# Indirect transfers tied one by one to TensorE's products, at the seam between a retention stage and a mixture of experts

## The chip, the core and the metric

The kernel runs on one core of a Trainium2 chip. The metric is device time of one execution in microseconds (us). The core has TensorE (PE, matrix products), VectorE (DVE), ScalarE (ACT), GpSimd (POOL) and SyncE (SP, which here issues DMAs); each runs its own instructions in order and waits on semaphores for the others.

## What is computed

Retention (a decaying causal attention) over 8 batches, 8 heads, 576 positions and 64 wide heads, then a mixture of 8 experts on its 4608 rows of 512, in which each row goes to the one expert with the largest gate.

```python
scores = np.matmul(q, k.transpose(0, 1, 3, 2)) / np.sqrt(64)
rel = pos[:, None] - pos[None, :]
Dmat = np.where(rel >= 0, gamma[:, None, None] ** rel[None], 0.0)     # gamma per head
x = rows(np.matmul(scores * Dmat, v))                                 # 4608 x 512
e_idx = np.argmax(x @ w_gate, axis=1)
gate_w = softmax(x @ w_gate)[chosen]; eom = sigmoid(x @ w_output_gate)
for e in range(8):
    mask = e_idx == e
    out[mask] = gate_w[mask, None] * eom[mask, e, None] * (np.maximum(x[mask] @ w1[e], 0) @ w2[e])
```

## The kernel before

The instructions of each engine stand in the order in which the code is written; a framework adds the semaphores.

**First stage.** A loop runs over 36 tiles of 128 rows (`g`). For a tile TensorE does, in this order: `scores(g + 1)` for the next tile (L439), sometimes `ranks` of a gate group (L529 to L536), `out_x(g)`, which is 16 products of the state with q (L470, here "state products") and then 16 of v with the masked scores (L473, "value products"), `update(g)` of the state (L456), `k_rows(g + 1)` (transposes of k, L417), and every fourth tile the `logits` of a group of four tiles (L491). ScalarE copies the results out (xT at L476, stT at L458, kn at L424), DVE masks the scores (L443) and transposes x for storing (L481).

Four tiles make a gate group `n`: DVE's `gate_a` (from L497 to L518, the one-hot of the chosen expert), then TensorE's `ranks`, DVE's `gate_b`, `gate_d`, `gate_c`. The last group's run behind the loop.

**GpSimd's list.** GpSimd prepares q (`prep_q`, L403) and v (`prep_v`, L410) of tiles some steps ahead. Between these it issues indirect DMAs: for every finished gate group four `scatter`s (L575, one for each tile, behind a small memset at L574), which write each token's entry into its expert's list `lst` in DRAM, and twelve `gather`s (L190), which fetch x of expert 0's first three token tiles (`w2h`, `w2l` are the buffers that they borrow) by the parts of the list that are already there. Scatters wait in a Python list `todo`; the tables `puts` and `mine` (L660, L661) say how many scatters and gathers are written into which tile's code; they have no tie to TensorE. In the expert stage, gathers (`paced`) wait for the product that was written last before them.

**The seam.** Behind the loop: logits of the last group, `store_x`, `load_idx(0, TA, TA + 1)` (SyncE's load L335 of a part of expert 0's list, which waits for all scatters so far), `gate_a` and `exp_a`, `mm1(0, 0, 0)`, which is the first of eight blocks of 12 products of expert 0 (L242), `ranks`, the rest of the gate, the last four scatters, `mm1(0, 0, 1)` and the sorting of the experts.

**Expert stage.** For each of 8 experts blocks `mm1` (L242) and `mm2` or `mm2t` (L263, L289), in float32 split into a high and a low part (three products for one). Results are written by GpSimd's indirect DMAs (L248).

Of the kernel before, what the change touches and what calls it, by code (L numbers as in the profile page):

```python
# [19 lines left out]
SYNC = mybir.DependencyInfo(mybir.DependencyClass.Sync, mybir.DependencyReason.DATA)  # L20
# [16 lines left out]
TA, CT = 3, 5  # L37
# [14 lines left out]
def tile_retention_moe(  # L52
# [126 lines left out]
        xps.append(a[:, 1].rearrange("p (k n) -> p k n", k=KB))  # L179
    pools = {"xt0": xta, "ht0": hpa}  # L180

    last = [None]

    def gather(e, t, u, paced=False):
        if u == 0 and e == 0 and t < TA:
            make_gidx(0, t, t + 1, G)
        if u == 0 and (e, t) not in XG:
            XG[e, t] = pools["xq"].tile([P, 4, P], F32, name="x_q")
        seen = xs if e or t >= TA else xs[0:4 * P * (READY[t] + 1) * GT]
        i = G.indirect_dma_start(out=XG[e, t][:, u, :], out_offset=None, in_=seen,  # L190
                                 in_offset=bass.IndirectOffsetOnAxis(ap=gidx[:, e, 4 * t + u:4 * t + u + 1], axis=0))
        if paced:
            tc.add_manual_dep(i.ins, last[0].name, SYNC, reason="one gather to a stretch of products")

    def size(e, part):
        return N1[e] if part else R0[e]
# [19 lines left out]
    def transp_a(e, t):  # L216
        src = xps.pop(0) if xps else pools["xq"].tile([P, KB, P], F32, name="x_t", bufs=2)
        nu = columns(e, t)
        V.transpose(out=src.rearrange("p k (u j) -> p u k j", u=4)[:, 0:nu],  # L219
                    in_=XG[e, t].rearrange("p u (k i) -> p u k i", k=KB)[:, 0:nu])  # L220
        part, c0, n = where(e, t)
        hi, lo = (a[:, :, c0:c0 + n] for a in xt_of(e, part))
        A.copy(out=hi, in_=src[:, :, 0:n])  # L223
        return lambda: V.tensor_tensor(out=lo, in0=src[:, :, 0:n], in1=hi.bitcast(F32), op=ALU.subtract)  # L224
# [236 lines left out]
    def out_x(g, S_sb, state):  # L461
        c = g % CPB
        o = o_ps[:, :, 256 * (g % 2):256 * (g % 2) + 256]
        part = lambda p, r: o[64 * ((p + r) % 2):64 * ((p + r) % 2) + 64, r, P * (p // 2):P * (p // 2) + P]
        order = [(p, (p + i) % 2) for p in range(NP) for i in range(2)]
        if state is not None:
            w = 64 if c == 4 else P
            for p, r in order:
                s = slice(64 * r, 64 * r + 64)
                T.matmul(part(p, r)[:, 0:w], lhsT=state[s, p, :], rhs=qs[g][s, p, 0:w],  # L470
                         start=(p < 2), stop=False, skip_group_check=True)
        for p, r in order:
            T.matmul(part(p, r), lhsT=vs[g][:, 2 * p + r, :], rhs=S_sb[:, r, p, :],  # L473
                     start=(state is None and p < 2), stop=True, skip_group_check=True)
        xT[g] = wk.tile([P, KB, P], F32, name="xT", bufs=6)
        A.copy(out=xT[g].rearrange("p (r s) i -> p r s i", r=2),  # L476
               in_=o[:, :, :].rearrange("p r (s i) -> p r s i", s=2))

    def x_rows(g):
        xq = xr[g] = wk.tile([P, 4, P], F32, name="xq", bufs=3)  # L480
        V.transpose(out=xq.rearrange("p b (r s i) -> p r s b i", r=2, s=2),  # L481
                    in_=xT[g].rearrange("p (r s) (b j) -> p r s b j", r=2, b=4))
# [81 lines left out]
    def gate_c(n):  # L564
        zs, sli = gt["zs"], gt["sli"]
        es = gt["ps"][:, 396:400].rearrange("p (t e) -> p t e", t=GT)
        V.tensor_reduce(out=es, in_=gt["ex"], op=ALU.add, axis=AX.X)
        V.tensor_scalar(out=es, in0=es, scalar1=1e-9, scalar2=None, op0=ALU.add)
        V.scalar_tensor_tensor(out=zs, in0=zs, scalar=1.0, in1=es, op0=ALU.add, op1=ALU.mult)
        ent = ents[:, n * GT:(n + 1) * GT]  # L570
        V.reciprocal(out=ent.bitcast(F32)[:, :, 1:2], in_=zs)  # L571

        def scatter(t):
            G.memset(tick, 0.0)  # L574
            i = G.indirect_dma_start(out=lst, out_offset=bass.IndirectOffsetOnAxis(ap=sli[:, t, :], axis=0),  # L575
                                     in_=ent[:, t], in_offset=None)
            tc.declare_no_dep(i.ins, group="lst", reason="the slots of all tokens differ")
            tc.add_to_no_dep_group("lst", i.ins)
            scat.append(i.ins)

        todo.extend(partial(scatter, t) for t in range(GT))
# [51 lines left out]
    for g in range(NTILE):  # L633
# [23 lines left out]
            ranks(n)  # L657
            exp_a(n)
        lead = 3 if g > 6 else 2
        puts = {16: 2, 17: 2, 18: 0, 19: 0, 24: 2, 25: 2, 27: 2, 28: 2, 30: 0, 31: 0, 35: 5}.get(g, 1)  # L660
        mine = {23: 1, 24: 1, 25: 1, 26: 1, 28: 1, 29: 2, 30: 1, 31: 1, 32: 1, 33: 2}.get(g, 0)  # L661
        while min(ready) < min(g + lead + 1, NTILE):
            if ready[0] <= ready[1]:
                prep_q(ready[0])
# [20 lines left out]
        out_x(g, S_sb, prev)  # L685
        if g == NTILE - 1:
            last_x = transp_a(0, 2)
        x_rows(g)
        if lows and late in (0, 3):
            lows.pop(0)()  # L690
# [22 lines left out]
    psctx.close()  # L713
    pools["ps_h"] = mctx.enter_context(tc.tile_pool(name="ps_h", bufs=5, space=PSUM, side="right", reuse_waits="tile"))
    store_x(NTILE - 1)
    load_idx(0, TA, TA + 1)
    gate_a(NG - 1)
    exp_a(NG - 1)
    mm1(0, 0, 0)
    ranks(NG - 1)  # L720
    gate_b(NG - 1)
    exp_b(NG - 1)
# [341 lines left out]
```

## Time and profile before

| | |
|---|---|
| median of 3 runs | 588.22 us (586.67 to 591.13) |
| profiled execution | 594.7 us, its span 592.6 us |
| TensorE (PE) busy | 558.9 us, 94% of the span |
| VectorE (DVE) busy | 367.0 us, 62% |
| GpSimd (POOL) busy | 329.7 us, 56% |
| ScalarE (ACT) busy | 179.0 us, 30% |
| mean granted TensorE clock | 0.980 |

Busy shares are means over both stages. The profile's rows give times from the start of the span. In a row of a timeline, the bracket at the end is the idle time of that engine just before the instruction and what released it: an instruction of another engine, "issue" where nothing that the profile shows was waited for, "remote" where a semaphore was waited for whose sender can't be named.

### The profile page before, as it was taken

The numbers are of one execution on the slowest core, as the hardware profiler recorded it, in microseconds if no ns is written. First come the engines' busy times: TensorE is split into PE (matmuls) and PEld (weight loads), VectorE is DVE, ScalarE is ACT, GpSimd is POOL, SyncE is SP. The second block draws the span as 40 slices with busy tenths as digits, with TensorE's granted clock in tenths as the row PEclk, the third lists the DMA queues.
The fourth block names the chain that finished last, engine by engine and source line by source line (L and its number), as shares of the span: only waits on it lengthen the run. The fifth ranks groups of instructions, "written<-read, shape, count | busy, mean of one in ns | idle before, by whom it ended". The sixth has DMA issues, their size and how long they took to land. (4 is left out here: it accounts for less than half of the span.)

```text
span 592.6 us, 14974 instructions
## 1 busy us (share of the span) xinstructions
PE 558.9 (94%) x5886; PEld 519.0 (88%) x5886; DVE 367.0 (62%) x805; ACT 179.0 (30%) x419; POOL 329.7 (56%) x359
## 2 busy tenths in 40 slices
PE   6989998999769989999999999999999999999994
PEld 4878887778569989998999899899999989999993
DVE  3668887678547465884576378457636747755440
ACT  4524435566114122420421232042123204213011
POOL 3848886889454576664555264345527526624602
PEclk9989998999879999999999999999999999999999
DMA  8989987796102475645643664464356455543123
GB/s 335 363 294 324 299 294 251 232 322 205 59 25 70 132 206 177 207 147 146 193 151 106 189 202 132 112 221 158 113 178 213 141 145 167 166 124 130 45 56 114
DMA packets 50069, 105.86 MB, mean 179 GB/s; under 512 B 10190, under 2 KB 24719, under 8 KB 49998
## 3 DMA queue, kind: packets, MB, share of 16 engines
q1 hardware_dynamic: 40254, 84.53, 44.8%
q0 software_dynamic: 9312, 19.71, 10.3%
q8 instruction: 47, 0.77, 0.5%
q10 hardware_dynamic: 432, 0.66, 0.4%
q14 instruction: 24, 0.20, 0.1%
HBM read 79.67 MB, written 25.33 MB: 177 GB/s over the span
## 5 line engine op out<-in xcount | busy, mean ns | idle before, releaser
L190 POOL DMA_INDIRECT x_q<-xs,gidx x139 | 149.4, 1075 | 90.2 <-PE y_ps L289 36.5
L242 PE MATMUL h_ps<-xh,w1h 128*128 128x256 f32 (+5 forms) x512 | 154.1, 301 | 0.4 <-DVE hl L245 0.4
L242 PE MATMUL h_ps<-xl,w1h 128*128 128x256 f32 (+5 forms) x512 | 153.9, 301 | 0.3 <-DVE xl L224 0.3
L242 PE MATMUL h_ps<-xh,w1l 128*128 128x256 f32 (+5 forms) x512 | 153.7, 300 | 0.0
L242 PEld LDWEIGHTS h_ps<-xh,w1h 128*128 128x128 f32 x512 | 97.2, 190 | 1.3 <-DVE hl L245 0.7
L242 PEld LDWEIGHTS h_ps<-xl,w1h 128*128 128x128 f32 x512 | 97.1, 190 | 0.8 <-DVE xl L224 0.5
L242 PEld LDWEIGHTS h_ps<-xh,w1l 128*128 128x128 f32 x512 | 97.9, 191 | 0.0
L244 ACT ACTIVATE hh<-h_ps 128x256 fp32r<-128x256 f32 (+5 forms) x128 | 52.4, 415 | 134.9 <-PE h_ps L242 110.0
L245 DVE SCALAR_TENSOR_TENSOR hl<-h_ps,hh 128x256 fp32r<-128x256 f32 (+5 forms) x128 | 57.8, 458 | 51.9 <-ACT hh L244 41.5
L289 PE MATMUL y_ps<-hh,w2l 128*128 128x360 f32 (+3 forms) x256 | 81.2, 317 | 0.0
L289 PE MATMUL y_ps<-hl,w2h 128*128 128x360 f32 (+3 forms) x256 | 81.2, 317 | 0.0
L289 PE MATMUL y_ps<-hh,w2h 128*128 128x360 f32 (+3 forms) x256 | 81.2, 317 | 0.0
L443 DVE TENSOR_TENSOR S_sb<-sc,cmat_sb 128x512 f32<-128x512 f32 x72 | 45.9, 679 | 22.7 <-PE sc L439 21.0
L223 ACT CAST xh<-x_t 128x512 fp32r<-128x512 f32 (+4 forms) x36 | 21.3, 592 | 122.3 <-DVE x_t L219 84.8
L224 DVE TENSOR_TENSOR xl<-x_t,xh 128x512 fp32r<-128x512 f32 (+4 forms) x36 | 23.8, 660 | 53.5 <-ACT xh L223 51.1
L248 POOL DMA_INDIRECT out_dram<-y,idx x15 | 15.3, 1018 | 67.1 <-ACT y L272 60.4
L248 POOL DMA_INDIRECT out_dram<-yr,idx x24 | 26.7, 1113 | 44.1 <-ACT yr L315 42.5
L439 PE MATMUL sc<-pk 64*64 64x64 f32 (+1 forms) x1152 | 38.4, 256 | 12.6 <-issue 7.2
L439 PEld LDWEIGHTS sc<-pk 64*64 64x64 f32 x1152 | 30.6, 139 | 21.5 <-issue 20.0
L167 DVE TENSOR_TENSOR w1l<-st,w1h 128x1024 fp32r<-128x1024 f32 (+1 forms) x36 | 47.9, 1330 | 2.1
L263 PE MATMUL y_ps<-w2h,hl 128*128 128x512 f32 x120 | 46.8, 390 | 2.0 <-DVE hl L245 2.0
L575 POOL DMA_INDIRECT lst<-ents,sli x36 | 37.0, 1029 | 20.6 <-DVE ents L571 15.0
(137 smaller groups left out, 970.1 us busy)
## 6 DMA issues: line engine op xcount, KB each, us to landing
st<-in_w_dram SPq DMA_DIRECT2D x64, 512.0 KB
pk<-in_pack_dram SPq DMA_DIRECT2D x35, 768.0 KB
xs<-xq SPq DMA_DIRECT2D x36, 256.0 KB
yr<-yg SPq DMA_DIRECT2D x16, 256.0 KB
yg<-yt SPq DMA_DIRECT2D x16, 176.0 KB
x_q<-xs,gidx POOLq DMA_INDIRECT x139
yg<-yt SPq DMA_DIRECT2D x12, 160.0 KB
yr<-yg SPq DMA_DIRECT2D x4, 208.0 KB
```

The lines of the kernel that those rows point to most:

```text
L167: V.tensor_tensor(out=lo[:, k], in0=st[:, k], in1=hi[:, k].bitcast(F32), op=ALU.subtract)
L190: i = G.indirect_dma_start(out=XG[e, t][:, u, :], out_offset=None, in_=seen, in_offset=bass.IndirectOffsetOnAxis(ap=gidx[:, e, 4 * t + u:4 ...
L224: return lambda: V.tensor_tensor(out=lo, in0=src[:, :, 0:n], in1=hi.bitcast(F32), op=ALU.subtract)
L242: last[0] = T.matmul(ps, lhsT=a[:, k, :], rhs=b[:, k, :], start=(j == 0), stop=(j == 3 * KB - 1)).ins
L244: A.activation(out=hh, in_=ps, func=AF.Relu)
L245: V.scalar_tensor_tensor(out=hl, in0=ps, scalar=0.0, in1=hh.bitcast(F32), op0=ALU.max, op1=ALU.subtract)
L248: i = G.indirect_dma_start(out=out, out_offset=bass.IndirectOffsetOnAxis(ap=rows, axis=0), in_=y, in_offset=None, bounds_check=NT - 1, oob ...
L263: last[0] = T.matmul(ps, lhsT=a[:, c0:c0 + n], rhs=b, start=(j == 0), stop=(j == 3 * FB - 1)).ins
L289: last[0] = T.matmul(ps[:, 0:n], lhsT=a, rhs=b, start=(j == 0), stop=(j == 3 * FB - 1)).ins
L439: T.matmul(sc[r][64 * h:64 * h + 64, p, i], lhsT=pk[g][s, 1, P * p + 64 * h:P * p + 64 * h + 64], rhs=qs[g][s, p, i], start=True, stop=Tru ...
L443: V.tensor_tensor(out=S_sb[:, r].rearrange("p (a b) i -> p a b i", a=2), in0=sc[r].rearrange("p (a b) i -> p a b i", a=2), in1=m, op=ALU.mult)
L575: i = G.indirect_dma_start(out=lst, out_offset=bass.IndirectOffsetOnAxis(ap=sli[:, t, :], axis=0), in_=ent[:, t], in_offset=None)
```

## The change

Three things are changed in the code.

- `gather` and `scatter` can be tied to a product: they then wait for its semaphore. `out_x` keeps its last state product as `marks["q"]` and its last value product as `marks["v"]`.
- The tables: a scatter more is written into tile 31 and none into tiles 33 to 35; the two gathers of tile 33 leave the table. Instead, behind `out_x(33)` come the two gathers, one tied to each mark, and behind `out_x(34)` and `out_x(35)` two scatters each, tied in the same way.
- Behind the loop, two scatters are issued from within `mm1(0, 0, 0)`, tied to its first and its seventh product, and `load_idx(0, TA, TA + 1)` stands behind that block. The four scatters of the last group are as before.

```diff
-    def gather(e, t, u, paced=False):
+    def gather(e, t, u, paced=False, by=None):
...
-        if paced:
-            tc.add_manual_dep(i.ins, last[0].name, SYNC, reason="one gather to a stretch of products")
+        if paced or by:
+            tc.add_manual_dep(i.ins, (by or last[0]).name, SYNC, reason="one gather to a stretch of products")
...
-                T.matmul(part(p, r)[:, 0:w], lhsT=state[s, p, :], rhs=qs[g][s, p, 0:w],
-                         start=(p < 2), stop=False, skip_group_check=True)
+                marks["q"] = T.matmul(part(p, r)[:, 0:w], lhsT=state[s, p, :], rhs=qs[g][s, p, 0:w],
+                                      start=(p < 2), stop=False, skip_group_check=True).ins
...
-            T.matmul(part(p, r), lhsT=vs[g][:, 2 * p + r, :], rhs=S_sb[:, r, p, :],
-                     start=(state is None and p < 2), stop=True, skip_group_check=True)
+            marks["v"] = T.matmul(part(p, r), lhsT=vs[g][:, 2 * p + r, :], rhs=S_sb[:, r, p, :],
+                                  start=(state is None and p < 2), stop=True, skip_group_check=True).ins
...
-        def scatter(t):
+        def scatter(t, by=None):
             G.memset(tick, 0.0)
...
+            if by:
+                tc.add_manual_dep(i.ins, (by[0] if by is last else by).name, SYNC,
+                                  reason="one scatter to a stretch of products")
...
-        puts = {16: 2, 17: 2, 18: 0, 19: 0, 24: 2, 25: 2, 27: 2, 28: 2, 30: 0, 31: 0, 35: 5}.get(g, 1)
-        mine = {23: 1, 24: 1, 25: 1, 26: 1, 28: 1, 29: 2, 30: 1, 31: 1, 32: 1, 33: 2}.get(g, 0)
+        puts = {16: 2, 17: 2, 18: 0, 19: 0, 24: 2, 25: 2, 27: 2, 28: 2, 30: 0, 33: 0, 34: 0, 35: 0}.get(g, 1)
+        mine = {23: 1, 24: 1, 25: 1, 26: 1, 28: 1, 29: 2, 30: 1, 31: 1, 32: 1}.get(g, 0)
...
         out_x(g, S_sb, prev)
         if g == NTILE - 1:
             last_x = transp_a(0, 2)
+        if g == 33:
+            gather(0, *divmod(got, 4), by=marks["q"])
+            gather(0, *divmod(got + 1, 4), by=marks["v"])
+        elif g > 33:
+            for m in "qv":
+                todo.pop(0)(by=marks[m])
         x_rows(g)
...
     store_x(NTILE - 1)
-    load_idx(0, TA, TA + 1)
     gate_a(NG - 1)
     exp_a(NG - 1)
-    mm1(0, 0, 0)
+    todo[:] = [partial(f, by=last) for f in todo]
+    mm1(0, 0, 0, (1, 7))
+    load_idx(0, TA, TA + 1)
     ranks(NG - 1)
```

The order of TensorE's, DVE's and ScalarE's instructions stays. On GpSimd, this stood between the preparation of tile 34 and that of the last gate (L403 and L410 are prep_q and prep_v of tile 35, L190 gathers, L575 scatters; the words in brackets are the semaphores waited for, PE for TensorE, DMASW for earlier indirect DMAs):

```order
L410 TENSOR_TENSOR pk<-pk,gkf 128x192
L403 TENSOR_TENSOR pk<-pk,gq_sb 128x512 [waits PE_49,Activation_49]
L190 DMA w2l_107<-xs,gidx 128x128 [waits DMASW1_49]
L410 TENSOR_TENSOR pk<-pk,gkf 128x192
L574 MEMSET tick 128x1
L575 DMA lst<-ents,sli 37888x16 [waits DMASW2_49,DVE_49]
L190 DMA w2l_107<-xs,gidx 128x128 [waits DMASW3_49]
L190 DMA w2l_107<-xs,gidx 128x128 [waits DMASW4_49]
L574 MEMSET tick 128x1 [waits Pool_49]
L575 DMA lst<-ents,sli 37888x16 [waits DMASW5_49]
```

and this stands there now:

```order
L410 TENSOR_TENSOR pk<-pk,gkf 128x192
L574 MEMSET tick 128x1
L575 DMA lst<-ents,sli 37888x16 [waits DMASW1_49,DVE_49]
L403 TENSOR_TENSOR pk<-pk,gq_sb 128x512 [waits PE_49,Activation_49]
L190 DMA w2l_107<-xs,gidx 128x128 [waits DMASW2_49]
L410 TENSOR_TENSOR pk<-pk,gkf 128x192
L574 MEMSET tick 128x1 [waits Pool_49]
L575 DMA lst<-ents,sli 37888x16 [waits DMASW3_49]
L190 DMA w2l_107<-xs,gidx 128x128 [waits DMASW4_49,PE_49]
L190 DMA w2l_107<-xs,gidx 128x128 [waits DMASW5_49,PE_49]
```

A scatter has moved ahead of prep_q of tile 35, and the two gathers of tile 33 now wait for TensorE as well.

Further down GpSimd's list, from the second of the scatters of tile 34 on, now tied (L559 is a small update of the list bases):

```order
L575 DMA lst<-ents,sli 37888x16 [waits DMASW7_49,PE_49]
L559 TENSOR_TENSOR base_81<-csm_sb,bump 128x1 [waits DVE_49]
L574 MEMSET tick 128x1 [waits Pool_49]
L575 DMA lst<-ents,sli 37888x16 [waits DMASW0_49,DVE_49,PE_49]
L574 MEMSET tick 128x1 [waits Pool_49]
L575 DMA lst<-ents,sli 37888x16 [waits DMASW1_49,PE_49]
L574 MEMSET tick 128x1 [waits Pool_49]
L575 DMA lst<-ents,sli 37888x16 [waits DMASW2_49,PE_49]
L574 MEMSET tick 128x1 [waits Pool_49]
L575 DMA lst<-ents,sli 37888x16 [waits DMASW3_49,PE_49]
```

The first of these five scatters belongs to tile 34, the next two to tile 35, the last two to `mm1(0, 0, 0)`. In the kernel before, the same five stood behind L559 with no wait for PE.

## Rows read from the trace of the kernel before

**Rows 1.** Busy time by stretch: stretch, us, PE, PEld, DVE, ACT, POOL busy, PEclk, DMA share, GB/s

```profile
177.00:592.60 415.60, 405.14 (x2636) 389.50 (x2634) 247.15 (x500) 99.50 (x205) 203.81 (x197) 1.00 0.49 148
150.90:157.00 6.10, 3.05 (x34) 1.78 (x34) 2.24 (x8) 1.00 (x3) 3.78 (x6) 0.95 0.22 68
162.80:171.10 8.30, 3.64 (x44) 2.93 (x45) 3.10 (x10) 1.61 (x4) 5.13 (x10) 0.94 0.13 47
171.10:176.90 5.80, 5.77 (x24) 5.72 (x24) 3.35 (x16) 0.68 (x2) 2.25 (x5) 0.50 0.03 7
```

**Rows 2.** PE's waits from 176.9 to the end, longest: total us, times, longest

```profile
PE y_ps L263 <- DVE hl L245: 2.0, 1, 2.0
```

**Rows 3.** PE in order of time: start us, us, line, operation, [idle before <-releaser]

```profile
109.55 1.09 PE L473 MATMUL o_ps<-S_sb,pk 128*64 128x128 f32 x16
...
115.80 1.09 PE L473 MATMUL o_ps<-S_sb,pk 128*64 128x128 f32 x16
...
148.81 1.11 PE L473 MATMUL o_ps<-S_sb,pk 128*64 128x128 f32 x16 [0.29 <-issue]
...
150.90 0.79 PE L439 MATMUL sc<-pk 64*64 64x128 f32 x12
152.10 0.32 PE L439 MATMUL sc<-pk 64*64 64x64 f32 x3 [0.41 <-issue]
...
156.48 0.56 PE L439 MATMUL sc<-pk 64*64 64x64 f32 x8 [0.99 <-issue]
156.97 0.21 PE L529 MATMUL lg_ps<-oh,cbf_sb 128*128 128x32 bf16 x1
...
158.29 1.82 PE L473 MATMUL o_ps<-S_sb,pk 128*64 128x128 f32 x16
...
161.70 1.09 PE L473 MATMUL o_ps<-S_sb,pk 128*64 128x128 f32 x16
...
165.28 0.39 PE L242 MATMUL h_ps<-xl,w1h 128*128 128x360 f32 x1
...
166.99 0.33 PE L242 MATMUL h_ps<-xh,w1l 128*128 128x360 f32 x1
171.13 0.18 PE L529 MATMUL lg_ps<-oh,cbf_sb 128*128 128x32 bf16 x1 [3.81 <-DVE oh L513]
```

**Rows 4.** ACT in order of time, the copy of tile 33's state

```profile
156.59 0.37 ACT L458 COPY stT<-st_ps 128x256 f32<-128x256 f32 x1 [4.61 <-remote]
```

**Rows 5.** DVE in order of time, ends and starts of gate_a

```profile
151.87 0.22 DVE L518 TENSOR_REDUCE oh<-oh 128x8 bf16<-128x40 bf16 x1
...
169.38 0.33 DVE L497 STREAM_TRANSPOSE lg_ps<-lg_ps 128x128 f32<-128x128 f32 x1 [4.20 <-remote]
```

**Rows 6.** POOL in order of time: the crowds' first and last transfers, and others

```profile
113.62 0.96 POOL L575 DMA_INDIRECT lst<-ents,sli  x1 [0.19 <-issue]
...
146.04 1.28 POOL L403 TENSOR_TENSOR pk<-pk,gq_sb 128x512 f32<-128x512 f32 x1
...
149.22 1.03 POOL L575 DMA_INDIRECT lst<-ents,sli  x1 [0.17 <-issue]
...
154.40 0.98 POOL L575 DMA_INDIRECT lst<-ents,sli  x1 [0.19 <-issue]
...
162.05 1.00 POOL L575 DMA_INDIRECT lst<-ents,sli  x1
...
167.61 0.97 POOL L575 DMA_INDIRECT lst<-ents,sli  x1 [0.19 <-issue]
...
186.77 0.98 POOL L190 DMA_INDIRECT x_q<-xs,gidx  x1 [0.30 <-issue]
```

**Rows 7.** SP's queue in order of time: the load of expert 0's list

```profile
169.90 0.56 SPq L335 DMA_DIRECT2D ls<-lst  x1
```

**Rows 8.** DMA queues in 150.9 to 157: packets, MB, share of 16 engines

```profile
q1 hardware_dynamic: 144, 0.26, 11.6%
q0 software_dynamic: 144, 0.15, 10.8%
```

More of the change, by code (lines that the diff above doesn't have):

```diff
@@ L180, in tile_retention_moe @@
     pools = {"xt0": xta, "ht0": hpa}
-    last = [None]
-    def gather(e, t, u, paced=False):
+    last, marks = [None], {}
+    def gather(e, t, u, paced=False, by=None):
         if u == 0 and e == 0 and t < TA:
```

## Prediction

> **What bounds the kernel now.** I read the stretches first. From 177.00 to the end of the span TensorE is busy for 405.14 of 415.60 us at the full granted clock [rows 1], and its longest wait there is 2.0 us [rows 2]. That part has hardly anything to give: whatever is won before 177 us arrives at the end one for one. The 27 us before it are another matter. In 150.90 to 157.00 TensorE is busy for half of the time, in 162.80 to 171.10 for less than half, and in 171.10 to 176.90 it works at a granted clock of 0.50 [rows 1].
>
> Next, TensorE in order of time [rows 3]. The value products of out_x (L473) mark the tiles: tile 34 begins them at 158.29, tile 33 at 148.81, so this tile took 9.48 us, where tile 35 took 3.41 (161.70 less 158.29). The lost time sits in scores(35), which began at 150.90 and dribbled on until after 156.48, with gaps (from 0.41 to 0.99) that the trace puts down to "issue": TensorE waits for nothing that is shown. The second loss is the 3.81 us before the rank products at 171.13, which wait for DVE's one-hot.
>
> What do the others do then? ScalarE's copy of the state starts at 156.59 after 4.61 us of waiting for something that the trace calls remote [rows 4], though the products that it copies stand in the program right behind tile 33's value products, which began at 148.81. DVE's first gate step (L497) starts at 169.38 after 4.20 us of the same kind [rows 5], though the logits, which it waits for, were through before expert 0's second product at 165.28 [rows 3]. So TensorE's own issue stalls, and what it has finished is heard late. GpSimd [rows 6] shows the company in which this happens: from 149.22 to 155.38 five indirect transfers of about 1 us follow one another with some 0.3 us between, and from 162.05 to 168.58 five more. Both times the delayed step starts 0.8 to 1.2 us after the crowd's last transfer ends (156.59 against 155.38, 169.38 against 168.58). A third case agrees: tile 25 took 6.25 us (109.55 to 115.80 in [rows 3]) with three transfers in it, of which the last [rows 6] follows the one before directly. My reading: a crowd of GpSimd's transfers holds up TensorE's issue and its signals while it lasts.
>
> **The change part by part.** No instruction is added or dropped except waits; the products stand in the same order. Eight scatters and two gathers get other places.
>
> *One scatter more goes ahead of the preparation of tile 35.* It pushes prep_q(35), at 146.04 [rows 6], back by one transfer, 1.3 us, so that it ends at 148.6. Scores(35) reads it at 150.90 [rows 3], so 2.3 us cover this. It costs nothing; without that cover it would cost 1.3 us.
>
> *Tile 33: two gathers tied to its products.* GpSimd is late here. Its list up to the first tied gather now takes one transfer more, so scatter and gathers run at about 150.5, 151.8 and 153.1 and end at 154.1 (149.22 in [rows 6] plus 1.3, then steps of 1.3, and 1.0 for the last). By then both products to which they are tied are long done. So the ties of tile 33 separate nothing: a crowd of three is left of five, since the two scatters behind it now wait for tile 34. Term A is what tile 34 saves. Best: the crowd of three does no harm; then the one-hot (DVE, 151.87 plus 0.22 [rows 5]) is the last to come, and ranks and state products take 1.32 (156.97 to 158.29), so the value products start at 153.4 instead of 158.29: 4.9 saved. Worst: the stall lasts until 1.1 us after 154.1, as it did after 155.38: about 1.3 saved. I take the tile with three transfers that the trace has, 6.25 us: 9.48 - 6.25 = 3.2 saved.
>
> *Tiles 34 and 35: four scatters, one after the state products and one after the value products of each.* Here GpSimd has nothing else to do, so each waits for its product; behind it in the queue stand only the other scatters and the small L559, whose reader is the last group's gate_b, after expert 0's first block. Tile 35 ran without any transfer (3.41 us) and now has two. The price of one: (6.25 - 3.41) / 3 = 0.95. Between nothing (they run beside products that need no signal) and 1.9, I take one of the two: 0.95 lost.
>
> *The last gate.* Of the five scatters at 162.05 to 168.58 one now belongs to tile 34, two to tile 35, and two go into expert 0's first block, behind its 1st and 7th product. Term B is what the last gate saves. Best: DVE starts L497 when it has finished its own work (165.2) instead of at 169.38. From there to the rank products it took 1.75 (169.38 to 171.13), so these could start at 167.15, when the first block has been issued, instead of 171.13: 4.0 saved. TensorE then doesn't stand still, and the 18 products that ran at a granted clock of 0.50 (24 less 6 rank products in [rows 1], 5.5 us, so 0.30 each) would take 0.17 each, as between 165.28 and 166.99 [rows 3]: 2.4 more. Worst: the transfer behind tile 35 and the two in the block make a new crowd, and nothing is saved. The first ends at about 164.4 in old time and the next can't begin before the block's first product has been heard; if the logits' signal slips out between them all is won, if it waits for that next one, which ends at 166.5, DVE starts 2 us later. I take the middle: 3.0 of 4.0, and 1.5 of 2.4 for the clock, 4.5 together.
>
> *The list load (L335) moved behind the first block.* It waited for the last scatter's landing anyway: it was issued at 169.90 [rows 7], 1.3 us after the end of the fifth at 168.58. It stays there relative to TensorE, costs nothing, and its reader comes in the fourth block of expert 0.
>
> Sum in the profiled execution: -3.2 + 0.95 - 4.5 = -6.8; with all best ends -11.3, with all worst ends +0.6. That execution took 594.7 us (span 592.6 and 2.1 around it), the three others 588.22 in the median, 6.5 less. If those 6.5 were all missing from the two stalls (11.3 at best), only 4.8 / 11.3 of my gain would be real, 2.9 us; if they are spread over the span, nearly all of it. Stalls of this kind stand in earlier tiles too, so I keep nine tenths: -6.2, that is **582.0 us**.
>
> One rule speaks against this reading. In 150.90 to 157.00 the DMA queues moved 144 packets of the ordinary queue and 144 of GpSimd's, and none of the instruction queues [rows 8]. The Trainium skill (Runtime: NRT & Kernel Launch, Instruction fetch mechanics) says that each engine's sequencer fetches its instructions in blocks with a DMA queue of its own while it works on the block before. By that rule a gap of "issue" would be a block that comes late; the trace doesn't agree for this gap, as no block moved.
>
> **The rivals.**
> 1. *The gaps are not the crowd's doing* (TensorE short of instructions, or a stall that only the profiled execution has). For it: the gaps have no releaser, and in the expert stage gathers follow one another at 0.30 us too (186.77 in [rows 6]) while TensorE has next to no waits [rows 2]. Against it: two engines start about 1 us after a crowd's end, twice, and no fetch moves [rows 8]. Then 588.2, within 586 to 590. Chance 0.23. The skill's fetch rule would end here too.
> 2. *Slower: every tied transfer starts just when the next signal is due.* The tie puts it behind a product, and so onto the signals of the value products, the state and the logits, where five of the old ones lay beside TensorE's waiting. Four in tiles 34 and 35 at 0.95 cost 3.8, tile 34 saves only 1.3, and the chain behind tile 35 ends 1 us later against the logits than before, with B at nothing: +3.5, 591.7. It decides once that chain holds the logits' signal for more than the 4.2 us of now. Against it: a tied transfer can't start before TensorE is heard, so the chain has to open between two. Chance 0.12.
> 3. *Only the last gate gains,* the three at tile 34 stalling it as five did, less 1.3: -1.3 + 0.95 - 4.5 = -4.85, 583.9 by the same nine tenths. This is inside my forecast's own range.
>
> **How the numbers follow.** The forecast with rival 3 has 0.65, with a range of its own from 578 to 586.5; rival 1 has 0.23, rival 2 0.12. For 8 in 10 the range takes rival 1 in and leaves out rival 2's upper part and the best ends: 578.0 to 589.5. One per cent, about what a measurement here can tell from no change, is 5.9 us: faster below 582.3, slower above 594.1. Of the forecast's 0.65 some 0.49 lie below 582.3 and the rest within; rival 1 is within; rival 2 gives 0.07 above and the rest within. So faster 0.49, within 0.44, slower 0.07.
>
> **What would show it.** Right: tile 34's pace near 6 us and no gap of "issue" in scores(35) past the third transfer; tied transfers at least a product's length apart in tiles 34 and 35; DVE's L497 within 1 to 2 us of the logits; ranks with under 1 us of idle; a granted clock near 1 from the second block on. Wrong: gaps in scores(35) with GpSimd silent (rival 1); tile 35 over 5 us, or L497 still 4 us behind the logits with the block's two scatters ahead of it (rival 2). The gathers of tile 33 landing late would show as DVE waiting at L219 for tile 2 of expert 0.

## The result, and the profile after

| | before | after |
|---|---|---|
| median in the same comparison (20 runs each) | 589.62 us (585.98 to 594.12) | 584.96 us (580.82 to 590.34) |
| profiled execution | 594.7 us, span 592.6 | 585.14 us, span 583.0 |
| TensorE busy in the span | 558.9 us | 554.0 us |
| granted clock | 0.980 | 0.988 |

The ratio after/before is 0.9919, with a 95% interval of 0.9893 to 0.9944: 0.8% less, 4.7 us, within the one per cent that the prediction called no change. (Ratios here are taken over undisturbed runs alone, so they need not be the ratio of two medians.)

TensorE of the changed kernel, in order of time (start us, us, line, operation, idle before and what released it), answers to [rows 3]:

```profile
144.33 1.09 PE L473 MATMUL o_ps<-S_sb,pk 128*64 128x128 f32 x16
146.41 0.90 PE L439 MATMUL sc<-pk 64*64 64x128 f32 x32
...
148.34 0.43 PE L470 MATMUL o_ps<-pk,stT 64*64 64x128 f32 x4 [0.34 <-issue]
149.11 0.44 PE L470 MATMUL o_ps<-pk,stT 64*64 64x128 f32 x4 [0.33 <-issue]
...
150.10 1.28 PE L473 MATMUL o_ps<-S_sb,pk 128*64 128x128 f32 x15
...
154.57 0.67 PE L470 MATMUL o_ps<-pk,stT 64*64 64x128 f32 x16 [2.62 <-ACT stT L458]
155.17 1.74 PE L473 MATMUL o_ps<-S_sb,pk 128*64 128x128 f32 x16
156.84 2.42 PE L491 MATMUL lg_ps<-xT,wg_sb 128*32 128x128 f32 x32
159.19 0.43 PE L242 MATMUL h_ps<-xh,w1h 128*128 128x360 f32 x1
...
161.27 0.19 PE L529 MATMUL lg_ps<-oh,cbf_sb 128*128 128x32 bf16 x1
161.44 0.41 PE L242 MATMUL h_ps<-xh,w1h 128*128 128x360 f32 x1
```

Read it by the value products (L473). Tile 34 took 150.10 - 144.33 = 5.77 us where it had taken 9.48; scores(35) at 146.41 has no gap any more, the gaps now stand in the state products. Tile 35 took 5.07 us, with a wait of 2.62 for the copy of the state. The rank products at 161.27 no longer wait (3.81 before), and the second block of expert 0 starts at 161.44, 17.11 us after tile 33's value products; before it was 171.42 - 148.81 = 22.61, where 148.81 stands in [rows 3] and 171.42 is this line of before:

```profile
171.42 0.65 PE L242 MATMUL h_ps<-xh,w1h 128*128 128x360 f32 x1
```

The rest of the 9.6 us between the two spans lies elsewhere: 4.5 of it is gone before tile 33's value products begin (148.81 against 144.33), in code that is almost the same in both kernels.

DVE's first gate step answers to [rows 5]. It now starts with the logits' signal, where it came 4.20 us behind a signal of unknown sender:

```profile
159.29 0.33 DVE L497 STREAM_TRANSPOSE lg_ps<-lg_ps 128x128 f32<-128x128 f32 x1 [0.54 <-PE lg_ps L491]
```

GpSimd answers to [rows 6]:

```profile
147.59 1.01 POOL L190 DMA_INDIRECT w2l<-xs,gidx  x1 [0.30 <-issue]
148.91 0.94 POOL L190 DMA_INDIRECT w2l<-xs,gidx  x1 [0.30 <-issue]
151.20 0.99 POOL L575 DMA_INDIRECT lst<-ents,sli  x1 [1.23 <-PE o_ps L470]
152.49 0.97 POOL L575 DMA_INDIRECT lst<-ents,sli  x1 [0.19 <-issue]
155.80 0.99 POOL L575 DMA_INDIRECT lst<-ents,sli  x1 [1.80 <-PE o_ps L470]
157.19 0.98 POOL L575 DMA_INDIRECT lst<-ents,sli  x1 [0.29 <-PE o_ps L473]
159.90 0.97 POOL L575 DMA_INDIRECT lst<-ents,sli  x1 [1.62 <-PE h_ps L242]
161.17 0.97 POOL L575 DMA_INDIRECT lst<-ents,sli  x1 [0.19 <-issue]
```

The six tied scatters did not come one by one. They came in pairs (0.19 to 0.29 us between the two of a pair): when a pair's first wait ends, the second product is nearly or quite done. Between pairs GpSimd waits 1.23 to 1.80 us, which I read as the openings through which the signals get out: the logits' own, at 159.29, falls between the end of a scatter at 158.17 and the start of the next at 159.90. In the second trace of this kernel (set 3) the two of tile 34 stood apart, the second after 0.76 us of waiting for the value products; the other two pairs came with 0.19 us again. There TensorE waited 0.53 us for the state instead of 2.62, and tile 35 took 3.55 us.

### The profile page after: what moved, and what is told of

Its sections match the earlier page's. It is cut to its first block, busy times and chain, and to the rows that moved or that the text cites. A ratio compares the mean times of both kernels' runs of the same rounds, so it can differ in the third digit from the quotient of the medians.

```text
span 583.0 us, 14980 instructions
## 1 busy us (share of the span) xinstructions
PE 554.0 (95%) x5886; PEld 514.1 (88%) x5886; DVE 363.8 (62%) x805; ACT 178.9 (31%) x419; POOL 328.9 (56%) x359
## 5 line engine op out<-in xcount | busy, mean ns | idle before, releaser
L190 POOL DMA_INDIRECT x_q<-xs,gidx x139 | 147.5, 1061 | 88.3 <-PE y_ps L289 32.6
L245 DVE SCALAR_TENSOR_TENSOR hl<-h_ps,hh 128x256 fp32r<-128x256 f32 (+5 forms) x128 | 57.6, 457 | 50.3 <-ACT hh L244 33.3
L263 PE MATMUL y_ps<-w2h,hl 128*128 128x512 f32 x120 | 48.1, 401 | 2.9 <-DVE hl L245 2.9
L289 PEld LDWEIGHTS y_ps<-hh,w2h 128*128 128x128 f32 x256 | 48.1, 188 | 0.6 <-issue 0.6
L575 POOL DMA_INDIRECT lst<-ents,sli x36 | 37.5, 1042 | 19.3 <-DVE S_sb L443 5.4
L289 PEld LDWEIGHTS y_ps<-hh,w2l 128*128 128x128 f32 x256 | 48.1, 188 | 0.0
L289 PEld LDWEIGHTS y_ps<-hl,w2h 128*128 128x128 f32 x256 | 48.1, 188 | 0.0
```

The lines of the kernel that those rows point to most:

```text
L245: V.scalar_tensor_tensor(out=hl, in0=ps, scalar=0.0, in1=hh.bitcast(F32), op0=ALU.max, op1=ALU.subtract)
L263: last[0] = T.matmul(ps, lhsT=a[:, c0:c0 + n], rhs=b, start=(j == 0), stop=(j == 3 * FB - 1)).ins
L289: last[0] = T.matmul(ps[:, 0:n], lhsT=a, rhs=b, start=(j == 0), stop=(j == 3 * FB - 1)).ins
```

## The experiments

The theory: a crowd of GpSimd's indirect transfers holds up TensorE's issue and its signals while it lasts. The rival: the gaps are TensorE's own (its instructions come late, or only the profile has them), and the crowd is mere company. The twelve runs were made in three sets of four; the first and the third set on one chip, here chip A, the second on another, chip B. Each median is of 12 runs (of 6 for the six left out in set 3), and the kernel before ran along in each set (35, 35 and 29 runs). The sets followed one another in the order A, B, A.

### Set 1: the parts, on chip A

*The kernel before, against itself.* 

> The kernel before once more, for a second profiled execution of it. If the 594.7 us of the first one was a slow draw, this one can be anywhere from 586 to 594, its tile 34 (the distance of the value products of tiles 33 and 34, 9.48 us in the first) and its idle time before the last ranks (3.81 us) differ from the first, and the whole time moves with them. If the profile itself costs the 6.5 us, it is 594 to 595 again with the same two stalls. The ratio of the timed runs is 1.00 by either.

*The ties alone.* The last two scatters go untied behind tile 35, and the list load goes back to its old place:

```diff
+    some(len(todo))
+    load_idx(0, TA, TA + 1)
     gate_a(NG - 1)
     exp_a(NG - 1)
-    todo[:] = [partial(f, by=last) for f in todo]
-    mm1(0, 0, 0, (1, 7))
-    load_idx(0, TA, TA + 1)
+    mm1(0, 0, 0)
```

> The ties in tiles 33 to 35 alone: the last two scatters stand untied behind tile 35, and the list load ahead of the gate as before. Crowding: tiles 34 and 35 as in the changed kernel (5.8 and 5.1 us), but three transfers now follow one another behind tile 35's value products, so DVE's L497 waits 2 to 3 us for the logits, the ranks find TensorE idle for 1.5 to 3 us: about 2 us under before, 587 to 588. Rival 1 (the gaps are not the transfers' doing): no difference to before, 589.6.

*The block alone.* The tables of before, but three scatters behind tile 35 instead of five; the other two tied in expert 0's first block:

```diff
-        puts = {16: 2, 17: 2, 18: 0, 19: 0, 24: 2, 25: 2, 27: 2, 28: 2, 30: 0, 33: 0, 34: 0, 35: 0}.get(g, 1)
+        puts = {16: 2, 17: 2, 18: 0, 19: 0, 24: 2, 25: 2, 27: 2, 28: 2, 30: 0, 31: 0, 35: 3}.get(g, 1)
-        mine = {23: 1, 24: 1, 25: 1, 26: 1, 28: 1, 29: 2, 30: 1, 31: 1, 32: 1}.get(g, 0)
+        mine = {23: 1, 24: 1, 25: 1, 26: 1, 28: 1, 29: 2, 30: 1, 31: 1, 32: 1, 33: 2}.get(g, 0)
-        if g == 33:
-            gather(0, *divmod(got, 4), by=marks["q"])
-            gather(0, *divmod(got + 1, 4), by=marks["v"])
-        elif g > 33:
-            for m in "qv":
-                todo.pop(0)(by=marks[m])
```

> The two scatters in expert 0's first block alone: the tables of before up to tile 34, three instead of five scatters in tile 35, untied, two tied in the block. Crowding: tile 34 as in the kernel before (7 to 9.5 us); behind tile 35 a crowd of three that ends 1 us after the logits, so L497 is 1 to 2 us late instead of 4 and the ranks' wait falls from 3.8 to about 1: 2 to 3 us under before. If it is the ties that bring the gain: no difference to before.

*The places without the ties.* The transfers stand where the changed kernel has them, no wait is added:

```diff
-        if paced or by:
-            tc.add_manual_dep(i.ins, (by or last[0]).name, SYNC, reason="one gather to a stretch of products")
+        if paced:
+            tc.add_manual_dep(i.ins, last[0].name, SYNC, reason="one gather to a stretch of products")
...
-            if by:
-                tc.add_manual_dep(i.ins, (by[0] if by is last else by).name, SYNC,
-                                  reason="one scatter to a stretch of products")
```

> The changed kernel with every transfer at its new place in GpSimd's list but without the ties. Crowding: scatter, two gathers and two scatters run as a crowd of five while tile 34's scores are due, as before (tile 34 at 8 to 9.5 us), and the four behind L559 as a second one that ends before the logits or with them; so the gain of tile 34 is lost and that of the gate partly kept: 586 to 589. If the places alone bring the gain: 585, as the changed kernel.

Measured: itself 588.72 us, ties alone 587.63, block alone 587.07, places alone 587.72; the kernel before in the same set 590.03. The ratios are 1.0042 (1.0001 to 1.0082), 0.9981 (0.9945 to 1.0016), 0.9968 (0.9932 to 1.0003) and 0.9987 (0.9947 to 1.0026). The first of them says how far a comparison can be off: a kernel against itself reads 0.4% away from one. So each part taken alone is worth 1.0 to 1.7 us against the copy, less than one set can tell for sure. Ties alone and block alone add up to 2.7 us where the whole change gives 4.7; with intervals of 0.4% to either side this does not show that the parts need each other. The traces say more than the times, and they are in the table below: with the places alone the crowd of five runs on at 0.2 to 0.3 us and hits tile 35 instead of tile 34 (7.25 us); with the ties alone the four behind tile 35, two tied and two not, still keep the gate's signal, and TensorE waits 1.83 us before the ranks; with the block alone that wait is gone, but tile 34 is as slow as before (6.64).

### Set 2: fewer transfers, on chip B

*The changed kernel again.* 

> The changed kernel once more, for a second profiled execution and five more rounds. Ratio to before 0.992 as measured. If the stalls vary from draw to draw, its tile 34 (5.77 us in the first profile), tile 35 (5.07) and ranks' wait (none) differ by 1 us or more; if the change has fixed them, they repeat within 0.3 us.

*Six left out.* The six tied scatters are dropped, and the loads of the lists expect six fewer:

```diff
-        assert len(scat) >= (NTILE if e or t0 > TA else GT * (READY[t0] + 1))
...
-            if len(scat) < NTILE:
+            if len(scat) < NTILE - 6:
...
-            for m in "qv":
-                todo.pop(0)(by=marks[m])
+            todo[0:2] = []
...
-    todo[:] = [partial(f, by=last) for f in todo]
-    mm1(0, 0, 0, (1, 7))
+    todo[:] = []
+    mm1(0, 0, 0)
```

> The changed kernel without the six scatters that it ties (four of tiles 34 and 35, two in the first block): the entries of six tiles miss in the lists, and their rows get no result. What it saves against the changed kernel is what these six still cost. Crowding, with each tied transfer holding a signal of TensorE's: tile 35 falls from 5.07 to about 3.5 us (no wait of 2.6 for the state), tile 34 stays at 5 to 6 by the three at its start: 2 to 3 us less than the changed kernel, 582 to 583. Rival: tied transfers cost nothing, the loss of tile 35 is chance: same as the changed kernel.

*One a tile.* One scatter, tied to the state products, in each of tiles 34 and 35; the other two join the second block:

```diff
-            for m in "qv":
-                todo.pop(0)(by=marks[m])
+            todo.pop(0)(by=marks["q"])
...
     mm1(0, 0, 0, (1, 7))
-    load_idx(0, TA, TA + 1)
...
-    some(len(todo))
-    mm1(0, 0, 1)
+    mm1(0, 0, 1, (1, 7))
+    load_idx(0, TA, TA + 1)
+    some(len(todo))
```

> One tied scatter a tile in 34 and 35 (behind the state products) instead of two; the other two go into expert 0's second block, and the list load behind that block. Crowding: no pair of transfers around tile 34's value products, so ScalarE gets the state in time and tile 35 takes 3.5 to 4 us instead of 5.07: 1 to 1.5 us less than the changed kernel. If the number of transfers in tiles 34 and 35 doesn't matter: the same as the changed kernel; if the later list load matters, it is slower, with DVE waiting for the list in expert 0's fourth block.

*None in the tiles.* All six in the first two blocks, behind products 1, 5 and 9 of each:

```diff
-        elif g > 33:
-            for m in "qv":
-                todo.pop(0)(by=marks[m])
...
-    mm1(0, 0, 0, (1, 7))
-    load_idx(0, TA, TA + 1)
+    mm1(0, 0, 0, (1, 5, 9))
...
-    some(len(todo))
-    mm1(0, 0, 1)
+    mm1(0, 0, 1, (1, 5, 9))
+    load_idx(0, TA, TA + 1)
+    some(len(todo))
```

> No scatter in tiles 34 and 35; three in each of expert 0's first two blocks, tied to their 1st, 5th and 9th product, and the list load behind the second. Crowding, with blocks of long products nearly insensitive: tile 35 at 3.5 us, the gate as in the changed kernel or up to 1 us later, since the block's first transfers come while the ranks' signal is due: 1 to 2.5 us less than the changed kernel, near the kernel with the six left out. If transfers cost the same wherever they stand: the same as the changed kernel.

Measured: 577.88, 577.92, 577.71 and 578.34 us, the kernel before in the same set 577.33. All four ratios lie between 0.9997 and 1.0023, with intervals of 0.3% to either side. On this chip the kernel before is 11 to 14 us faster than on chip A, the changed one 7 and the one without the six scatters 3 (set 3 has these for chip A), and neither the change nor leaving the six scatters out shows in the time. So what was expected of the six left out, of one a tile and of none in the tiles did not come, and none of the three says how chip A would answer. The trace of the changed kernel on chip B shows why. TensorE first, then GpSimd's first and last transfer of the stretch, then DVE's transpose of what the last gathers brought:

```profile
144.93 0.90 PE L439 MATMUL sc<-pk 64*64 64x128 f32 x32 [0.66 <-POOL pk L403]
...
146.00 0.67 PE L470 MATMUL o_ps<-pk,stT 64*64 64x128 f32 x16
146.59 1.09 PE L473 MATMUL o_ps<-S_sb,pk 128*64 128x128 f32 x16
148.68 0.67 PE L470 MATMUL o_ps<-pk,stT 64*64 64x128 f32 x16 [0.53 <-ACT stT L458]
149.28 1.09 PE L473 MATMUL o_ps<-S_sb,pk 128*64 128x128 f32 x16
...
154.17 0.67 PE L242 MATMUL h_ps<-xh,w1h 128*128 128x360 f32 x1 [2.06 <-ACT xh L223]
```

```profile
147.17 1.03 POOL L575 DMA_INDIRECT lst<-ents,sli  x1 [0.16 <-issue]
...
157.54 0.97 POOL L575 DMA_INDIRECT lst<-ents,sli  x1 [0.19 <-issue]
```

```profile
152.83 0.71 DVE L219 STREAM_TRANSPOSE w2l<-w2l 128x512 f32<-128x512 f32 x1 [2.75 <-DMA w2l<-xs,gidx]
```

Nine transfers follow one another from 147.17 to 158.51, longer than the crowds of chip A's traces in this stretch (five before, eight with six doubled), and TensorE runs through it: tile 35 takes 2.69 us, no row from 142 to 160 has a gap of "issue", the state comes at once. What TensorE waits for here is GpSimd's work itself: 0.66 us for the prepared q and 2.06 us for the last gathers' rows. In all four traces of chip B expert 0's first block waits for these rows (2.02 to 2.27 us), also with the six left out; so the equal times alone would not show that the crowd does nothing there. The missing gaps do: the crowd is there, its effect on TensorE is not.

### Set 3: the dose, on chip A

*The kernel before.* 

> The kernel before once more, with a trace of its own, on one chip with the three below. Crowd theory, in two forms that the trace tells apart: (a) this chip stalls TensorE during crowds, as in the traces of before, after and of the first four experiments: before near 590 us, gaps of issue of 0.2 to 1.0 us among the products of tile 34, the last gate's L497 two or more us behind the logits, ranks waiting 1 to 4 us for the one-hot. (b) this chip doesn't, as in the four traces of the second call: before near 577, tiles 34 and 35 without a gap of issue, L497 not waiting, and TensorE waiting instead for POOL's pk and for tile 2's xh ahead of expert 0's first block. Rival (the gaps belong to the order of the program, and before has them on any chip): before slow with gaps even where after has none, so over 1% between the two in either case.

*The changed kernel.* 

> The changed kernel once more, same chip. Crowd theory: in case (a) 3 to 6 us under before (ratio 0.990 to 0.995), of it 2 to 3 us between the value products of tile 33 and the first product of expert 0's second block, and the rest in the granted clock of the first block's neighbourhood; in case (b) within 0.3% of before. Rival: 4 to 6 us under before on either kind of chip. A theory by which the first comparison was luck: within 0.3% on either.

*Six left out,* the edit of set 2. 

> The changed kernel without the six tied scatters (six tiles' tokens are missing in the lists, so their rows get no expert's result; all products still run). It gives what spreading could win at most. Crowd theory: (a) another 2 to 4 us under the changed kernel, tile 35 back at 3.4 us from 5.1, logits at 1.1 us instead of 2.4, since nothing is in flight there; the gaps behind tile 33's two gathers stay. (b) the same as the changed kernel within 0.3%. Rival (instruction supply alone): the gaps stay in tiles 34 and 35 although nothing is in flight, and the time stays on any chip.

*Six doubled.* Each tied scatter is followed by another of the same entries into a spare table:

```diff
+    spare = dram.tile([E * NR, 16], I32, name="spare")
...
+            if by:
+                G.memset(tick, 0.0)
+                i = G.indirect_dma_start(out=spare, out_offset=bass.IndirectOffsetOnAxis(ap=sli[:, t, :], axis=0),
+                                         in_=ent[:, t], in_offset=None)
...
```

> The changed kernel with each of the six tied scatters followed by a second one of the same entries into a spare table that nobody reads: six more transfers of about 1.3 us on GpSimd, the same products. Crowd theory: (a) tile 35 grows by another 1 to 2 us, the state of tile 35 and the last gate's signals are heard 1 to 3 us later, in all 2 to 5 us over the changed kernel (ratio to it 1.003 to 1.009). (b) TensorE shows nothing of it in tiles 34 and 35; the last gate's own scatters and the list load come up to 5 us later, which its reader in the fourth block of expert 0 covers: within 0.3% of the changed kernel. Rival: within 0.3% on any chip.

| tied scatters | none | six (changed) | twelve | before, its copy |
|---|---|---|---|---|
| median us | 581.17 | 584.79 | 594.23 | 590.03 |
| ratio to before (591.61) | 0.9847 | 0.9898 | 1.0067 | 0.9986 |
| 95% interval | 0.9788 to 0.9906 | 0.9862 to 0.9935 | 1.0032 to 1.0101 | 0.9948 to 1.0024 |

TensorE's products are the same in all four, only transfers differ, and the time follows them: six cost 3.6 us, six more 9.4, which is about twice the upper end that was expected. The first step is the less certain one. The intervals of none and six overlap, and so do the runs themselves (579.17 to 585.96 against 581.74 to 588.63); by their spread I estimate the 3.6 to be good to 2 or 3 us. Twelve against six is clear of that. The stretch from 150 to 172 us in three traces (stretch, us, then PE, PEld, DVE, ACT and POOL busy, granted clock, DMA share, GB/s); with none:

```profile
150.00:172.00 22.00, 20.81 (x196) 19.08 (x197) 18.64 (x69) 9.71 (x18) 6.31 (x11) 1.00 0.19 68
```

with six (the trace of this set):

```profile
150.00:172.00 22.00, 18.46 (x195) 16.45 (x196) 14.87 (x57) 7.19 (x16) 12.29 (x23) 0.92 0.17 50
```

with twelve:

```profile
150.00:172.00 22.00, 16.01 (x147) 14.20 (x147) 10.10 (x39) 4.76 (x11) 13.70 (x26) 0.84 0.11 35
```

TensorE's busy time and its granted clock fall together as GpSimd's busy time grows. With none in flight tile 35 is quick and DVE starts on the logits (156.78) without an idle time; tile 34 keeps its 5.78 us, since scatter and gathers of tile 33 are still there:

```profile
144.78 1.09 PE L472 MATMUL o_ps<-S_sb,pk 128*64 128x128 f32 x16
...
148.72 0.44 PE L469 MATMUL o_ps<-pk,stT 64*64 64x128 f32 x4 [0.32 <-issue]
...
150.56 1.36 PE L472 MATMUL o_ps<-S_sb,pk 128*64 128x128 f32 x16
...
153.50 1.09 PE L472 MATMUL o_ps<-S_sb,pk 128*64 128x128 f32 x16
```

With twelve, DVE hears the logits 3.46 us late (L498 is L497 there), while from 157.28 to 167.53 eight transfers run with 0.2 to 0.3 us between:

```profile
162.46 0.33 DVE L498 STREAM_TRANSPOSE lg_ps<-lg_ps 128x128 f32<-128x128 f32 x1 [3.46 <-PE h_ps L243]
```

That trace accounts for some of the 9.4 us: the second block starts 20.50 us after tile 33's value products, 3.4 to 3.8 later than in the two traces of the changed kernel, and TensorE then waits another 1.8 us between 184 and 198, 0.8 for the low part of weights and 1.0 for gathered rows; SyncE's later loads of expert 0's list began at 180.63 there, in the first trace of the changed kernel at 173.84. So a part of the second step is GpSimd's own list running later, not TensorE held up by a crowd, and the two are not separated. The rest is not shown: this execution (589.98 us) was the fastest of its kernel.

All traces side by side, in us: from the value products (L473) of tile 33 to those of 34, from there to 35, from there to the first product of expert 0's second block, and the sum; then from there to the end of the span.

| kernel, chip | tile 34 | tile 35 | to 2nd block | sum | to the end |
|---|---|---|---|---|---|
| before, first trace | 9.48 | 3.41 | 9.72 | 22.61 | 421.2 |
| before, set 1, A | 6.59 | 4.38 | 8.85 | 19.82 | 419.9 |
| before, set 3, A | 7.34 | 5.17 | 10.34 | 22.85 | 419.0 |
| after, first trace | 5.77 | 5.07 | 6.27 | 17.11 | 421.6 |
| after, set 3, A | 6.70 | 3.55 | 6.49 | 16.74 | 418.5 |
| ties alone, A | 5.56 | 5.18 | 8.38 | 19.12 | 417.5 |
| block alone, A | 6.64 | 5.23 | 6.97 | 18.84 | 419.1 |
| places alone, A | 4.76 | 7.25 | 8.16 | 20.17 | 417.2 |
| six left out, A | 5.78 | 2.94 | 5.51 | 14.23 | 419.3 |
| six doubled, A | 5.43 | 5.67 | 9.40 | 20.50 | 423.7 |
| after, set 2, B | 4.47 | 2.69 | 8.79 | 15.95 | 419.1 |
| six left out, B | 5.16 | 2.68 | 9.06 | 16.90 | 418.9 |
| one a tile, B | 5.14 | 2.68 | 9.18 | 17.00 | 418.4 |
| none in the tiles, B | 5.70 | 2.68 | 9.43 | 17.81 | 419.3 |

The mean sum is 21.8 for three traces of before and 16.9 for two of after (which chip the first trace of either kernel is from isn't known; both have chip A's gaps). The difference, 4.8 us, agrees with the measured gain (4.7 in the first comparison, 5.2 against the copy in set 3). The means are of few traces, and single ones differ by up to 3 us. Ahead of the table's first column the changed kernel is 0.6 us earlier in the mean, and the last column is 420.0 in the mean for either, of which more below.

## Why the prediction came out as it did

**What bounds the kernel.** Right in the main: the 4.8 us won before the second block are there at the end too, by the means. How evenly the rest runs shows behind the second block's first 24 products: from there to the end it takes 414.7, 414.4 and 414.7 us in the traces of before, 414.5 in one of the changed kernel, and 417.5 in the other. That one is the exception, and it comes below.

**The mechanism.** Right on chip A, and shown there by the dose (none, six, twelve). Rival 1, by which the gaps are not the crowd's doing, falls there: with TensorE's products the same, 13 us lie between none and twelve, and the traces show 6.3 of them between tile 33 and the second block (14.23 against 20.50). In a gap of the changed kernel the queues again moved no block of instructions (set 3, 149.9 to 152.6, where four gaps of 0.24 to 0.53 stand):

```profile
q1 hardware_dynamic: 144, 0.26, 25.2%
q0 software_dynamic: 43, 0.10, 17.4%
```

So the rule of the Trainium skill (Runtime: NRT & Kernel Launch, Instruction fetch mechanics), that the sequencer fetches its instructions by a DMA queue of its own, names nothing here that was late. But on chip B rival 1 describes what happens: crowds without gaps, and a change that doesn't show. The prediction had taken the mechanism for the kernel's; it belongs to the kernel and the chip together.

**Tile 34 (term A, -3.2).** The value after came out as forecast: 6.25 was taken from tile 25, and 5.77 and 6.70 came, 6.24 in the mean. The value before was not right: 9.48 was the worst of three traces, with 6.59 and 7.34 in the others, 7.80 in the mean. So the term was -1.6. This is the step that was furthest off: a stall that changes from one execution to the next was priced by the one execution that had been profiled, which was 6.5 us slower than the median. The value products of tiles 33 and 34 in the two other traces of before, of set 1 and of set 3:

```profile
145.01 1.09 PE L473 MATMUL o_ps<-S_sb,pk 128*64 128x128 f32 x16
...
151.60 2.54 PE L473 MATMUL o_ps<-S_sb,pk 128*64 128x128 f32 x15
```

```profile
144.98 1.09 PE L473 MATMUL o_ps<-S_sb,pk 128*64 128x128 f32 x16
...
152.32 0.83 PE L473 MATMUL o_ps<-S_sb,pk 128*64 128x128 f32 x4
```

That 6.25 fitted has some luck in it, for tile 25 is not like tile 34. It holds the logits of a group as well, about 1 us of products in the first trace of before:

```profile
111.62 1.08 PE L491 MATMUL lg_ps<-xT,wg_sb 128*32 128x128 f32 x32
```

The trace of before in set 1 has a tile with logits and without a gap, from 140.66 to 145.01: 4.35 us.

```profile
140.66 1.09 PE L473 MATMUL o_ps<-S_sb,pk 128*64 128x128 f32 x16
...
142.73 1.08 PE L491 MATMUL lg_ps<-xT,wg_sb 128*32 128x128 f32 x32
```

**Tiles 34 and 35 tied (term +0.95).** 5.07 and 3.55 after, against 3.41, 4.38 and 5.17 before: 4.31 and 4.32 in the mean, so nothing was lost. Again the value after (3.41 + 0.95 = 4.36) was right and the one trace of before was an outlier, this time a quick one. The price of a transfer is there all the same: without any, the tile takes 2.94. But the 0.95 was worked out from unlike tiles, as tile 35 has neither logits nor a next tile's scores. Against the 4.35 of a like tile, three transfers cost (6.25 - 4.35) / 3 = 0.63 each, near the 0.6 that the dose gives (3.6 / 6).

**The last gate (term B, -4.5).** 3.0 of it was to come up to the second block: 9.64 before in the mean (9.72, 8.85, 10.34), 6.38 after, so -3.3. The 1.5 for the clock behind it came as well: the second block's first 24 products take 6.50, 5.46 and 4.23 us before, 4.03 and 3.93 after, 1.4 less in the mean. The granted clock stands at 0.50 for about 10, 6 and 17 us of the stretch from 150 to 177 in the three traces of before, for about 3 us in either trace of the changed kernel (in its first one that is tile 35 and the logits, which then take 2.42 instead of 1.08 us). That the way from the second block to the end is no shorter, 420.0 us for both, comes from the first trace of the changed kernel alone. There TensorE waits for the low part of hidden values (hl, L245) longer than in the others (0.99 to 2.01 before, 1.70 in set 3), and from 210 to 225 the granted clock is 0.77:

```profile
210.83 0.79 PE L263 MATMUL y_ps<-w2h,hl 128*128 128x512 f32 x1 [2.87 <-DVE hl L245]
```

Whether that wait grows because TensorE comes to it earlier is not shown.

**Sum and factor.** By the means of the traces -1.6 + 0 - 3.3 - 1.4 = -6.3 up to the second block's 25th product, where the prediction had -6.8; 1.5 of it is lost again behind, in one trace of two. So the sum is close because errors cancel: A was 1.6 too large, the tied transfers 0.95 too dear. The factor of nine tenths (which makes -6.1 of -6.8, not -6.2) answered to the slow profile and was put on all terms alike. That execution was slow in other places: of the 6.8 us by which its span exceeds the mean of the two others, 3.8 lie ahead of tile 33's value products, 1.3 between them and the second block (tile 34 had 2.5 too much, tile 35 1.4 too little) and 1.7 behind. The kernel before took 589.62 in the comparison instead of 588.22, and so the time came out 3 us above the 582.0: 1.4 of it is the base, 1.5 the gain. It lies in the class to which the prediction gave 0.44, with 0.49 for the one below.

**The rivals.** Rival 3, with tile 34 at -1.3 and everything else as forecast, gave -4.85 in the profile and 583.9: nearest to what came, but not for its reason. Tile 34 did fall to 6.24 after; what was smaller was the value before. Rival 2 (slower, as tied transfers start just when a signal is due) did not decide, because the pairs left openings; but six doubled comes close to that rival, with the logits heard 3.46 us late and 0.7% over before.

**The signs.** Tile 34 near 6 us: yes. No gap past the third transfer: yes in the first trace; in set 3's the last gap, 0.53 us, ends at 152.40, 0.80 after that transfer's end. Tied transfers a product's length apart: no, but for the two of tile 34 in set 3 they came in pairs. Tile 35 over 5 us, a sign of rival 2: in the first trace (5.07), not in the other (3.55). L497 within 1 to 2 us of the logits: yes (0.54 and 1.51 us of waiting). Ranks with under 1 us of idle: none in one trace, 1.13 in the other. A granted clock near 1 from the second block on: yes up to 210 us in the first trace. The extra scatter ahead of prep_q(35) and the moved list load cost nothing on chip A, as said: scores(35) waits for no q, and the load was issued at 163.45:

```profile
163.45 0.55 SPq L335 DMA_DIRECT2D ls<-lst  x1
```

On chip B scores(35) does wait for q, 0.66 to 1.89 us in the four traces; whether the extra scatter is the cause isn't shown, since the kernel before has no trace there.

**Left open.** Why chip A has the stalls and chip B has not is not known; two chips were seen, one core of each. Nor is it known what in a transfer holds TensorE and its signals up: the runs vary how many there are and where, and nothing else about them. No trace of the kernel before was taken on chip B, so that the change is worth nothing there rests on its times alone.

## What to carry to other kernels

When TensorE shows short gaps that nothing releases, and other engines hear its results late, look at what GpSimd transfers at that moment: on one of the two chips seen here six such transfers, in pairs, cost about 3.6 us, four of them beside short products and two in the block before the last ranks; twelve, in longer crowds, cost far more. Leave openings behind the products whose signal is awaited, and put no crowd ahead of a gate. That long products are the better place is likely from the last row below, but the kernel that moved all six there (none in the tiles) ran on chip B alone, where nothing showed. Price a stall by several executions, on more than one chip and against a tile that does the same work: a single profile had one term twice too large, and unlike tiles made a transfer half too dear.

## What the hardware showed that was not expected

**Two chips, two behaviours.** The same program took 577.33 us in the median on one chip and 590.03 and 591.61 on the other. From 100 to 160 us the traces on chip A show 10 to 15 gaps of "issue" on TensorE, those on chip B 1 to 3.

**A beat.** During a crowd the short products come in small lots at an even step. In set 3's trace of the changed kernel the scores start at 150.16, 150.91 and 151.65 and the ranks at 152.40: a step of 0.75 us, in which 1 to 3 of the scores' products are issued, besides weight loads and some others.

```profile
150.16 0.33 PE L439 MATMUL sc<-pk 64*64 64x64 f32 x3 [0.24 <-issue]
150.91 0.31 PE L439 MATMUL sc<-pk 64*64 64x64 f32 x3 [0.43 <-issue]
151.65 0.21 PE L439 MATMUL sc<-pk 64*64 64x64 f32 x1 [0.43 <-issue]
152.40 0.19 PE L529 MATMUL lg_ps<-oh,cbf_sb 128*128 128x32 bf16 x1 [0.53 <-issue]
```

**Long products ran on.** In the first trace of the changed kernel the last four scatters run from 165.00 to 170.72 beside expert 0's products of 360 columns, and TensorE is busy all the time at the full granted clock (stretch, us, PE, PEld, DVE, ACT, POOL busy, clock, DMA share, GB/s):

```profile
163.00:171.00 8.00, 8.00 (x50) 8.00 (x50) 7.28 (x32) 4.75 (x8) 5.15 (x7) 1.00 0.21 43
```

It is not separated whether their length is the reason, or that fewer instructions are issued in a microsecond.
